# Batch 0's q and k in halves of the tokens, v's loads moved in the issue order, and the last block's two products swapped

## The chip, the cores and the metric

The kernel runs on one core of one Trainium2 chip. The metric is device time in microseconds, the median of several executions. The engines are TensorE (PE; its weight loads are PEld), VectorE (DVE), ScalarE (ACT), GpSimd (POOL) and SyncE (SP); each takes its own instructions in order. All loads are issued by GpSimd, because they convert float32 to bfloat16 on the way; nearly all stores are issued by SyncE.

## What is computed

Sliding-window attention with a linear bias for 8 batches, 8 heads, 576 tokens and 64 channels, and behind it a highway layer on the 4608 tokens of width 512:

```
scores = q k^T / 8 - slope[h] * |i - j|      for 0 <= i - j < 128, else masked
attn   = softmax(scores) v                   8 x 8 x 576 x 64
x      = attn as [8*576, 512]
H      = relu(x w_h);  T = sigmoid(x w_t + b_t)
out    = T * H + (1 - T) * x                 float32
```

## The kernel before

**Units and blocks.** A batch's attention is cut into 4 units of 128 keys (the last has 192), 32 units in all. Tokens go through the highway layer in 36 blocks of 128: four per batch, and one more for each pair of batches, made of the two remainders of 64.

**Steps.** The kernel is a list of small steps, written out by hand in the string `ORDER` (lines 28 to 37): each letter is a step, and the n-th occurrence of a letter is its n-th unit, block or load in the lists that `lists()` gives. The order of the letters is the order of the instructions on every engine; there are no loops beside it.

- `L`, `load`: one DMA issue on GpSimd. q and k of a batch go to the tiles `LD` (3 buffers of each), v to `VA`. Batch 0's q and k come in two parts each (the even and odd partitions, `j`), those of the others in four. v is one load per batch. The weights come in four parts each. The loads are in one list; at most 8 seem to be under way at a time: the ninth behind a load waits for it.
- `T`, `tr`: VectorE's 32 x 32 transposes of a batch's q (w = 0) or k (w = 1) from `LD` to `TR`.
- `V`, `copy_v`: two copies of v by VectorE to the other half of the partitions (`VC`).
- `s`, `scores`: TensorE; `e`, `soft`: ScalarE's exponent; `m`, `mask`: for eight of the units VectorE multiplies with a mask instead of adding it by matmuls.
- `p`, `pv`: attention times v on TensorE, with the sums in a column of ones; `n`, `norm`: VectorE's reciprocal and product; `x` and `c`: TensorE's transposition and ScalarE's copy.
- `h`, `mm_h`, and `z`, `mm_z`: the two products with the weights. `b`: ScalarE puts the bias into z's PSUM bank ahead of it; for the first and the last block a matmul does that.
- `u`, `relu_sub`: relu(h) - x in one step of VectorE from PSUM; or, for blocks in `RELU_S`, `r`, `relu`, on ScalarE and then `v`, `sub`, on VectorE from two-byte data.
- `a`: ScalarE's tanh; `y`: VectorE's scaling to the gate; `g`: the product with the gate; `o`, `add_x`: GpSimd adds x (for the last three blocks VectorE does, `f`); `d`: the store.
- `W`: TensorE multiplies zeros at the start. The digits are parts of the setup; `2` counts positions on GpSimd, `3` makes the bias, `4` the identity, `7` a copy of the bias for the batches' last units, `8` and `9` the mask.

VectorE's steps on two-byte data in SBUF (`m`, `V`, `v`, `y`, `g`) go through `locked`, and `add_x` on GpSimd waits for the last such step ahead of it in the order (`after`). Loads have no such wait.

PSUM has one buffer each for scores, P·V, h and z.

Of the kernel before, what the change touches and what calls it, by code (L numbers as in the profile page):

```python
# [9 lines left out]
P = 128  # L10
NB, NS = 8, 4
NLD, NTR, NVA, NVC, NP = 3, 3, 5, 3, 8


RELU_S = (5, 7, 8, 10, 11, 13, 14, 15, 16, 17, 19, 20, 22, 23, 25, 26, 28, 29, 31, 32, 33, 34, 35)
BIAS_S = (1, 2, 3, 4, 5, 6, 7, 8, 9, 10, 11, 12, 13, 14, 15, 16, 17, 18, 19, 20, 21, 22, 23, 24, 25, 26, 27, 28, 29, 30, 31, 32, 33, 34)

SUM_S = []
# [7 lines left out]
MASK_V = (1, 5, 9, 13, 17, 21, 25, 29)  # L26

ORDER = (
    "1LL62L3LL8L9LL7TLLLLTWWWWWWWWWseWWWWsLVeL4WWWpLsmLLneLWWWxLcLWWpsLnLLxhcepLuzLnLTLxahL5c"
    "bpTzyasgubonehLdxuLcsyLVzeLpnasLmLxhcLgbLpueLznLhTaLoxscbdupeznyxThcapbnrzgxoscapeLdhnLb"  # L30
    "VxscuLpezLnLhaLmLbxsTLrLczehygapvobsnrydxgzTcopayLdhbnLezyVxscyLvayLubLgpLeggLznLhoaTbxs"
    "ocdpeznodasmdbrvxTzchagyoprbhnedzguoxascVLdbpLeLznTaxscLbLpeLhvnzryyxvahycybprsnhegvzvoT"
    "rxasLdcgbpghenozmdrxasgocbpyLdeznLLhTaLxLrscbpezonxaydhvcVbpusnzeyxyhgcgmoapsrbodnhexvLd"
    "zgLcvLgpavLsrnobheyLdTxLzcLuopahnbLdzvrLyyxyaysVcbpgehonTrxdzcpasbnhegxyzgocupavdsvobnhe"
    "dmxzgcyropasndyxThcbpgrgzegonhoadxuscbVdpezonhaydyvbxvscyrpzenhgvmoxrscagdpgbhonezuodxas"
    "vcdybgpgeyohnzrodxahvdcgbpyorzndgaxvhcobprzdnyaxvhbygcgzorfhavddzyrgfavdygfd"
)

PARTS = [(2,) if b < 1 else (0, 1) for b in range(NB)]
WP, VP = 4, 1


def lists():

    units = [(b, s) for b in range(NB) for s in range(NS)]
    blocks = []
    for m in range(NB // 2):
        blocks += [(b, s) for b in (2 * m, 2 * m + 1) for s in range(NS)] + [(2 * m, NS)]  # L50
    trs = [(b, w) for b in range(NB) for w in range(2)]
    loads = []
    for b in range(NB):
        loads += [("t", b, w, j, i) for w in range(2) for j in range(2) for i in PARTS[b]]
        if b == 0:
            loads += [("v", 0, i) for i in range(VP)]
            loads += [("w", w, i) for w in (1, 0) for i in range(WP)] + [("w", 2, 0)]
        else:
            loads += [("v", b, i) for i in range(VP)]
# [12 lines left out]
    by["W"] = [()] * 100  # L72
    by["b"] = [n[i] for i in n if i in BIAS_S]
    return by
# [3 lines left out]
def kernel(  # L78
# [10 lines left out]
    nc = tc.nc  # L89
    B, H, S, D = q.shape  # L90
# [6 lines left out]
    U32 = mybir.dt.uint32  # L97
# [7 lines left out]
    NT = S // 16  # L105
# [13 lines left out]
    LD = {(i, w): cp.tile([P, NT, D], BF16, name=f"ld{i}{w}")  # L119
          for i in range(NLD) for w in range(2)}  # L120
# [22 lines left out]

    BL = cp.tile([P, 4, 384], BF16, name="bl")

    def load(kind, *at):
        if kind == "t":
            b, w, j, i = at
            n, i = (4, 0) if i == 2 else (2, i)
            nc.gpsimd.dma_start(  # L150
                out=LD[b % NLD, w][64 * i + j : 64 * i + 32 * n : 2].rearrange(
                    "p t d -> p (t d)"),
                in_=(q, k)[w][b, 4 * j + 2 * i : 4 * j + 2 * i + n].rearrange(
                    "g (s t) d -> (g s) (t d)", t=NT))
        elif kind == "v":
            b, i = at
            m = slice(36 // VP * i, 36 // VP * (i + 1))
            nc.gpsimd.dma_start(
                out=VA[b % NVA][:, m, 0:D],
                in_=v[b].rearrange("h s d -> (h s) d").rearrange("(m p) d -> p m d", p=P)[:, m])  # L160
        elif at[0] < 2:
            w, i = at
            c = slice(NC // WP * i, NC // WP * (i + 1))
            nc.gpsimd.dma_start(
                out=(wH, wT)[w][:, c, :],
                in_=(moe_w_h, moe_w_t)[w].rearrange("(c p) n -> p c n", p=P)[:, c, :])
# [65 lines left out]
        nc.tensor.matmul(out=pb[:], lhsT=ones0[:], rhs=bT[:], start=True, stop=True)  # L232
        nc.scalar.copy(out=bB[:], in_=pb[:])

    def tr(b, w):

        nc.vector.transpose(  # L237
            out=TR[b % NTR, w][:].rearrange("p n e -> p (n e)").bitcast(U32).rearrange(
                ("p (j s t) -> p t s j", "p (s t j) -> p t s j")[w], j=2, t=NT),
            in_=LD[b % NLD, w][:].rearrange("p t d -> p (t d)").bitcast(U32).rearrange(  # L240
                "p (t i) -> p t i", i=32))

    SC, PT, AV, RD, X = {}, {}, {}, {}, {}
# [177 lines left out]
    def mm_z(*at):  # L421
        begun = at in PZ
        if not begun:
            if lists()["z"].index(at) in LATE:
                PZ[at] = ps_sc.tile([P, G, 512], F32, name="sc")[:, 0, :]
            else:
                PZ[at] = ps_z.tile([P, DM], F32, name="z")[:]
            nc.tensor.matmul(out=PZ[at], lhsT=ones0[:], rhs=bT[:], start=True, stop=False)
        xt = XT[at]
        for c in range(NC):  # L430
            nc.tensor.matmul(out=PZ[at], lhsT=xt[:, c, :], rhs=wT[:, c, :],  # L431
                             start=False, stop=c == NC - 1, skip_group_check=begun)
# [39 lines left out]
    def store(b, s):  # L472
        ot = OT.pop((b, s))
        for i in range(1 + (s == NS)):
# [49 lines left out]
```

## Time and profile before

| | us |
|---|---|
| time, median of 3 runs | 159.09 (158.67 to 159.47) |
| the profiled execution | 160.06 |
| its span, first to last instruction | 158.3 |
| PE busy | 134.1 |
| DVE busy | 127.6 |
| ACT busy | 121.2 |
| POOL busy | 89.5 |

A row of the timeline gives start, length, engine, line, operation and names, the number of instructions that were merged into it, and in brackets the idle time of the engine before it with what ended it. A row of the chain of waits gives start, length and what the end of the program was waiting for in that time.

### The profile page before, as it was taken

The numbers are of one execution on the slowest core, as the hardware profiler recorded it, in microseconds if no ns is written. First come the engines' busy times: TensorE is split into PE (matmuls) and PEld (weight loads), VectorE is DVE, ScalarE is ACT, GpSimd is POOL, SyncE is SP. The second block draws the span as 40 slices with busy tenths as digits, with TensorE's granted clock in tenths as the row PEclk, the third lists the DMA queues.
The fourth block names the chain that finished last, engine by engine and source line by source line (L and its number), as shares of the span: only waits on it lengthen the run. The fifth ranks groups of instructions, "written<-read, shape, count | busy, mean of one in ns | idle before, by whom it ended". The sixth has DMA issues, their size and how long they took to land.

```text
span 158.3 us, 6992 instructions
## 1 busy us (share of the span) xinstructions
PE 134.1 (85%) x3096; PEld 73.7 (47%) x3096; DVE 127.6 (81%) x252; ACT 121.2 (77%) x176; POOL 89.5 (57%) x115
## 2 busy tenths in 40 slices
PE   0579897969997999699997999899699999999930
PEld 0114453544564565345654654465455555655310
DVE  5761629889949999998868589699999888997990
ACT  8353646677778979699988997987799698998730
POOL 7940967595249369926905592499404370766400
PEclk9999999999999999999999999999999999999996
DMA  3999999999969999996998589989993231145252
GB/s 57 168 161 178 203 197 139 182 233 156 183 164 147 169 201 203 169 200 215 193 157 135 149 148 157 136 188 220 201 175 117 93 133 70 72 137 197 73 201 66
DMA packets 46462, 25.09 MB, mean 159 GB/s; under 512 B 38752, under 2 KB 39776, under 8 KB 46432
## 3 DMA queue, kind: packets, MB, share of 16 engines
q0 software_dynamic: 41184, 15.21, 89.9%
q1 hardware_dynamic: 5168, 9.31, 16.9%
q8 instruction: 24, 0.39, 1.0%
q10 hardware_dynamic: 80, 0.13, 0.2%
q14 instruction: 6, 0.05, 0.1%
HBM read 30.41 MB, written 9.44 MB: 252 GB/s over the span
## 4 chain that ended last, share of the span: by engine, by line
PE 36%; DVE 31%; ACT 9%; issue 9%; DMA 6%; POOL 5%; DVEq 0%; POOLq 0%
PE h L398 10%; PE z L431 9%; DMA ld<-in_k_dram 6%; PE av L345 6%; DVE x L366 6%; DVE tr L237 6%; DVE tt L439 4%; DVE uu L443 4%; PE sc L302 4%; DVE uu L413 4%; ACT p L314 3%; PE av L380 3%; ACT xt L385 3%; DVE vc L321 3%; DVE uu L403 2%
## 5 line engine op out<-in xcount | busy, mean ns | idle before, releaser
L449 POOL TENSOR_TENSOR ot<-uu,x 128x512 f32<-128x512 bf16 x33 | 38.6, 1177 | 50.1 <-issue 16.6
L314 ACT ACTIVATE p<-sc 128x1536 bf16<-128x1536 f32 x32 | 46.5, 1452 | 7.1 <-PE sc L266 4.9
L398 PE MATMUL h<-wH,xt 128*128 128x512 bf16 x144 | 37.1, 380 | 0.5 <-DVE uu L403 0.3
L431 PE MATMUL z<-wT,xt 128*128 128x512 bf16 x140 | 36.1, 380 | 0.5 <-ACT z L419 0.3
L237 DVE STREAM_TRANSPOSE tr<-ld 128x1152 uint32<-128x1152 uint32 x16 | 29.4, 1850 | 2.3 <-DMA ld<-in_k_dram 1.5
L385 ACT COPY xt<-av 128x512 bf16<-128x512 bf16 x36 | 21.0, 583 | 11.1 <-PE av L380 10.9
L366 DVE TENSOR_TENSOR x<-av,rd 128x512 bf16<-128x512 f32 x36 | 24.9, 692 | 4.3 <-POOL ot L449 1.2
L345 PEld LDWEIGHTS <-p 64*128 64x128 bf16 (+1 forms) x1088 | 18.7, 96 | 16.2 <-issue 12.9
L436 ACT ACTIVATE tt<-z 128x512 f16<-128x512 f32 x35 | 21.0, 600 | 6.2 <-PE z L431 5.5
L345 PE MATMUL av<-va,p 64*128 64x65 bf16 (+1 forms) x544 | 21.5, 191 | 3.0 <-ACT xt L385 1.8
L345 PE MATMUL av<-vc,p 64*128 64x65 bf16 (+1 forms) x544 | 21.5, 192 | 0.8 <-DVE vc L321 0.8
L302 PE MATMUL sc<-tr,tr 32*64 32x192 bf16 (+2 forms) x1152 | 20.1, 254 | 2.4 <-DVE tr L237 1.2
L419 ACT COPY z<-bB 128x512 f32<-128x512 f32 x34 | 20.4, 599 | 0.4
L398 PEld LDWEIGHTS <-xt 128*128 128x128 bf16 x144 | 12.5, 97 | 13.5 <-issue 2.0
L431 PEld LDWEIGHTS <-xt 128*128 128x128 bf16 x144 | 12.5, 97 | 12.9 <-issue 0.9
L380 PE MATMUL av<-ident,x 128*128 128x128 bf16 x144 | 14.1, 221 | 4.9 <-DVE x L366 3.2
L302 PEld LDWEIGHTS <-tr 32*64 32x64 bf16 x1152 | 14.6, 136 | 7.3 <-issue 2.4
L150 POOL DMA_DIRECT2D ld<-in_k_dram x30 | 15.7, 535 | 3.9 <-DMA wH<-in_moe_w_h_dram 1.4
L380 PEld LDWEIGHTS <-x 128*128 128x128 bf16 x144 | 9.5, 97 | 17.2 <-DVE x L366 13.2
L443 DVE TENSOR_TENSOR uu<-uu,tt 128x512 bf16<-128x512 bf16 x36 | 16.4, 476 | 0.3
L150 POOL DMA_DIRECT2D ld<-in_q_dram x30 | 15.8, 548 | 1.0 <-POOLq L508 0.8
L365 DVE RECIPROCAL rd<-av 128x8 f32<-128x8 f32 x36 | 7.2, 201 | 10.6 <-PE av L345 10.4
(50 smaller groups left out, 136.3 us busy)
## 6 DMA issues: line engine op xcount, KB each, us to landing
out_dram<-ot SPq DMA_DIRECT2D x32, 256.0 KB, 2.5
va<-in_v_dram POOLq DMA_DIRECT2D x8, 576.0 KB, 10.8
ld<-in_q_dram POOLq DMA_DIRECT2D x28, 144.0 KB, 8.8
ld<-in_k_dram POOLq DMA_DIRECT2D x28, 144.0 KB, 5.6
out_dram<-ot SPq DMA_DIRECT2D x7, 128.0 KB, 3.7
ld<-in_q_dram POOLq DMA_DIRECT2D x2, 288.0 KB, 4.4
ld<-in_k_dram POOLq DMA_DIRECT2D x2, 288.0 KB, 6.6
wT<-in_moe_w_t_dram POOLq DMA_DIRECT2D x4, 128.0 KB, 9.6
```

The costliest lines, as they stand in the source:

```text
L150: nc.gpsimd.dma_start(out=LD[b % NLD, w][64 * i + j : 64 * i + 32 * n : 2].rearrange("p t d -> p (t d)"), in_=(q, k)[w][b, 4 * j + 2 * i : ...
L237: nc.vector.transpose(out=TR[b % NTR, w][:].rearrange("p n e -> p (n e)").bitcast(U32).rearrange(("p (j s t) -> p t s j", "p (s t j) -> p ...
L302: nc.tensor.matmul(out=sc[j * D : (j + 1) * D, g, off : off + n], lhsT=KT[rows, a * D : (a + 1) * D, j, e], rhs=QT[rows, a * D : a * D + n ...
L314: nc.scalar.activation(out=t[:, :, :, 0:192], in_=SC.pop((b, s))[:, :, 0:384].rearrange("p g (i n) -> p g i n", i=2), func=ACTF.Exp, scale ...
L345: nc.tensor.matmul(out=av[o : o + n, j, g * (D + 1) : (g + 1) * (D + 1)], lhsT=PT[bb, ss][rows, g].rearrange("p i n -> p (i n)")[:, at : a ...
L366: nc.vector.tensor_tensor(out=x[:].rearrange("p (j g d) -> p j g d", j=2, d=D), in0=av[:, :, :, 0:D], in1=rd[:].to_broadcast([P, 2, G, D]) ...
L380: nc.tensor.transpose(out=x_part(at)[:, c // 2, (c % 2) * P : (c % 2 + 1) * P], in_=X[at][:, c * P : (c + 1) * P], identity=ident[:])
L385: nc.scalar.copy(out=xt[:].rearrange("p (j c) n -> p j (c n)", j=2), in_=x_part(at))
L398: nc.tensor.matmul(out=pa, lhsT=xt[:, c, :], rhs=wH[:, c, :], start=c == 0, stop=c == NC - 1)
L431: nc.tensor.matmul(out=PZ[at], lhsT=xt[:, c, :], rhs=wT[:, c, :], start=False, stop=c == NC - 1, skip_group_check=begun)
L443: locked(nc.vector.tensor_tensor(out=UU[at][:], in0=UU[at][:], in1=TT.pop(at)[:], op=ALU.mult))
L449: op = nc.gpsimd.tensor_tensor(out=ot[:], in0=uu[:], in1=x[:], op=ALU.add)
```

## The change

1. Batch 0's q and k are loaded in two halves of the tokens each (288 tokens, `SPLIT = (0, 1)`); the second halves land in the buffers `LD[2, w]`, which are free then. The load order is first half of q, first half of k, v, second half of q, second half of k, then the bias of z, then the weights. Each half has its own transposes (`tr` takes a third index, and the list `T` has 18 entries instead of 16).
2. `ORDER` is new as a whole. At the start the identity (`4`) comes ahead of the bias (`3`), ten zero matmuls come ahead of the mask, and the copy `7` behind the first exponent. The issues of v for batches 2 to 7 stand at other places among VectorE's steps.
3. For the last block z comes ahead of h, and block 35 leaves `RELU_S`: its relu and subtraction are one step of VectorE (`u`), ahead of the product `g`, instead of `r` on ScalarE and `v` on VectorE.

```diff
-RELU_S = (5, 7, 8, 10, 11, 13, 14, 15, 16, 17, 19, 20, 22, 23, 25, 26, 28, 29, 31, 32, 33, 34, 35)
+RELU_S = (5, 7, 8, 10, 11, 13, 14, 15, 16, 17, 19, 20, 22, 23, 25, 26, 28, 29, 31, 32, 33, 34)
...
 ORDER = (
-    "1LL62L3LL8L9LL7TLLLLTWWWWWWWWWseWWWWsLVeL4WWWpLsmLLneLWWWxLcLWWpsLnLLxhcepLuzLnLTLxahL5c"
-    "bpTzyasgubonehLdxuLcsyLVzeLpnasLmLxhcLgbLpueLznLhTaLoxscbdupeznyxThcapbnrzgxoscapeLdhnLb"
...
-    "vcdybgpgeyohnzrodxahvdcgbpyorzndgaxvhcobprzdnyaxvhbygcgzorfhavddzyrgfavdygfd"
+    "1LL26L43LLLTWWWWWWWWWW8LLTL9LLWWWsLeLV7LWWWWpLTLnWWWsLTexLLcsmLLpeLznLLLLxasc5pbLhnezuLx"
+    "ahLcTLbLzLLpaLTusyghneouxdcsyLyVheLpbnsLmLxzcLuLpagLhnbLeozuTxdscabypeznTaxhcbgpryyoznsa"
...
+    "bpuezndhgayyoxrscgdbpveohnydxgzgcorpahnobdrxyzdvcgpoahnbdyrxvzgcfzavdyhgafydugfd"
 )
...
-WP, VP = 4, 1
+WP, VP, SPLIT = 4, 1, (0, 1)
...
-    trs = [(b, w) for b in range(NB) for w in range(2)]
...
+    half = [(3, 4) if w in SPLIT else (2,) for w in range(2)]
+    trs = [(0, w, half[w][0]) for w in range(2)] + [(0, w, i) for w in range(2) for i in half[w][1:]]
+    trs += [(b, w, 2) for b in range(1, NB) for w in range(2)]
+    loads = [("t", 0, w, j, half[w][0]) for w in range(2) for j in range(2)]
+    loads += [("v", 0, i) for i in range(VP)]
+    loads += [("t", 0, w, j, i) for w in range(2) for i in half[w][1:] for j in range(2)]
+    loads += [("w", 2, 0)] + [("w", w, i) for w in (1, 0) for i in range(WP)]
+    for b in range(1, NB):
         loads += [("t", b, w, j, i) for w in range(2) for j in range(2) for i in PARTS[b]]
...
+        loads += [("v", b, i) for i in range(VP)]
...
+    def part(b, w, i):
+
+        return LD[b % NLD, w][:] if i < 3 else LD[2 * (i - 3), w][:, 0 : NT // 2]
+
     def load(kind, *at):
         if kind == "t":
             b, w, j, i = at
+            if i > 2:
+                rows = slice((i - 3) * S // 2, (i - 2) * S // 2)
+                nc.gpsimd.dma_start(
+                    out=part(b, w, i)[j:P:2].rearrange("p t d -> p (t d)"),
+                    in_=(q, k)[w][b, 4 * j : 4 * j + 4, rows].rearrange(
+                        "g (s t) d -> g s (t d)", t=NT // 2))
+                return
...
-    def tr(b, w):
-
+    def tr(b, w, i):
+
+        n, h = (1, 0) if i < 3 else (2, i - 3)
         nc.vector.transpose(
             out=TR[b % NTR, w][:].rearrange("p n e -> p (n e)").bitcast(U32).rearrange(
-                ("p (j s t) -> p t s j", "p (s t j) -> p t s j")[w], j=2, t=NT),
-            in_=LD[b % NLD, w][:].rearrange("p t d -> p (t d)").bitcast(U32).rearrange(
+                ("p (j h s t) -> p h t s j", "p (h s t j) -> p h t s j")[w],
+                j=2, h=n, t=NT // n)[:, h],
+            in_=part(b, w, i).rearrange("p t d -> p (t d)").bitcast(U32).rearrange(
                 "p (t i) -> p t i", i=32))
```

In the new order the copy of v of batch 1 still stands ahead of the issue of v of batch 2. The rows around the issues of v, as the two orders have them on VectorE (numbers are units for `m`, blocks otherwise): before, `V1` / issue 2; `n8` / issue 3 / `V2`; `n11` / issue 4 / `y6 V3`; `n14` / issue 5 / `n15`; `T60` / issue 6 / `n20`; `n24` / issue 7 / `y19 y20`. After, `V1` / issue 2 / `n4`; `V2` / issue 3 / `u6 n8`; `u9` / issue 4 / `V3`; `T50` / issue 5 / `n16`; `T60` / issue 6 / `u18`; `V6` / issue 7 / `n26`.

More of the change, by code (lines that the diff above doesn't have):

```diff
@@ L28 @@
 ORDER = (
-    "1LL62L3LL8L9LL7TLLLLTWWWWWWWWWseWWWWsLVeL4WWWpLsmLLneLWWWxLcLWWpsLnLLxhcepLuzLnLTLxahL5c"
-    "bpTzyasgubonehLdxuLcsyLVzeLpnasLmLxhcLgbLpueLznLhTaLoxscbdupeznyxThcapbnrzgxoscapeLdhnLb"
[L31 to L35, printed above, removed]
-    "vcdybgpgeyohnzrodxahvdcgbpyorzndgaxvhcobprzdnyaxvhbygcgzorfhavddzyrgfavdygfd"
+    "1LL26L43LLLTWWWWWWWWWW8LLTL9LLWWWsLeLV7LWWWWpLTLnWWWsLTexLLcsmLLpeLznLLLLxasc5pbLhnezuLx"
+    "ahLcTLbLzLLpaLTusyghneouxdcsyLyVheLpbnsLmLxzcLuLpagLhnbLeozuTxdscabypeznTaxhcbgpryyoznsa"
+    "gLdVLbLxhcepuzLnLaLTxsocbphednzrvxmscavpybyhnezggrgoxTscLdpevLyhnLLasgLubLxezhcVLapLbson"
+    "rzeTodxhcodapsnrLdbLmxzcvvpayyhnbezyuxghcgToasbLdpeLznLLrxTLascbpehonzrgLdgxLahyVLcLbpLr"
+    "znoaxscydvobpehndzgrvmoxascbvdpvezyynhaggxrsTocbpLdvezLnLhTaLxscbopeuzndhaVbxsycyyrypzen"
+    "hyggxamoscbpgdrvozenhodTaxsLcdubLvpLeghLnozryLxdagsLgcgLbvpLeznoxahVLdcbprznohTaodbxscdp"
+    "euznhayyxmscrvpybhenzgvrToxascbdypgeoznhaydgbxouscpgdeohnsrvdVzevxhgcmapsnobrzvdyxgahyco"
+    "bpuezndhgayyoxrscgdbpveohnydxgzgcorpahnobdrxyzdvcgpoahnbdyrxvzgcfzavdyhgafydugfd"
 )
 PARTS = [(2,) if b < 1 else (0, 1) for b in range(NB)]
-WP, VP = 4, 1
+WP, VP, SPLIT = 4, 1, (0, 1)
 def lists():
@@ L50, in lists @@
         blocks += [(b, s) for b in (2 * m, 2 * m + 1) for s in range(NS)] + [(2 * m, NS)]
-    trs = [(b, w) for b in range(NB) for w in range(2)]
-    loads = []
-    for b in range(NB):
-        loads += [("t", b, w, j, i) for w in range(2) for j in range(2) for i in PARTS[b]]
[L55 to L59, printed above, removed]
+    half = [(3, 4) if w in SPLIT else (2,) for w in range(2)]
[6 more added lines that the diff above has]
+    for b in range(1, NB):
+        loads += [("t", b, w, j, i) for w in range(2) for j in range(2) for i in PARTS[b]]
+        loads += [("v", b, i) for i in range(VP)]
     by = dict(L=loads, T=trs, V=list(range(NB)))
```

## The prediction

> **What bounds the kernel now.** I read the page first, then the chain of waits over the first 36 us, then the timeline of single engines at the start, around three of the v issues and at the end. The page:
>
> ```profile
> span 158.3 us, 6992 instructions
> PE 134.1 (85%) x3096; PEld 73.7 (47%) x3096; DVE 127.6 (81%) x252; ACT 121.2 (77%) x176; POOL 89.5 (57%) x115
> ...
> PE   0579897969997999699997999899699999999930
> ...
> PE 36%; DVE 31%; ACT 9%; issue 9%; DMA 6%; POOL 5%; DVEq 0%; POOLq 0%
> ```
>
> No engine alone sets the time. The chain alternates between TensorE and VectorE, and each is busy over 80% of the span. The holes are at the start, where TensorE has three poor slices (4 us each), and at the end. The profiled execution took 160.06 us: its span and 1.76 around it. That is 0.97 over the median, 159.09, of the three timed runs; I work out differences on the trace and take them off 159.09.
>
> The chain of waits for the first 36 us (start, us, what):
>
> ```profile
> 3.61 7.06 DMA ld<-in_k_dram
> ...
> 12.20 0.87 PE sc L302 x31
> ...
> 16.11 1.46 ACT p L314
> ...
> 17.62 0.59 PE sc L302 x28
> ...
> 29.43 0.51 PE sc L302 x29
> ...
> 30.27 0.98 PE h L398 x4
> ...
> 32.18 0.47 DVE vc L321
> ...
> 32.67 1.86 DVE vc L321
> ...
> 34.58 0.41 PE av L345 x15
> ```
>
> Three things set the first third. The first scores wait for all of k of batch 0 (10.67). From 12.2 to 31.25 the chain is TensorE's and ScalarE's own work. Then the first P·V of batch 1, unit 4 (I call it p4), waits for the copies of v, of which the second took 1.86 us where the first took 0.47. The timeline of GpSimd says why:
>
> ```profile
> 15.61 0.53 POOL L164 DMA_DIRECT2D wH<-in_moe_w_h_dram  x1 [4.12 <-DMA va<-in_v_dram]
> ...
> 31.89 0.51 POOL L150 DMA_DIRECT2D ld<-in_k_dram  x1 [0.48 <-DMA va<-in_v_dram]
> 32.38 1.85 POOL L158 DMA_DIRECT2D va<-in_v_dram  x1
> ```
>
> GpSimd waits until v of batch 1 has landed (31.87), issues the last part of k of batch 2, and at 32.38 begins the issue of v of batch 2, 1.85 us. VectorE's copy that starts after 32.38 ends only after 34.23. The copy that had started before it, at 32.18, kept its 0.47 us across 32.38. So an issue of v holds two-byte steps that start behind it, and not one already running.
>
> **Part 1, batch 0 in halves.** The rows of VectorE and TensorE at the start:
>
> ```profile
> 4.97 1.15 DVE L207 SCALAR_TENSOR_TENSOR bt<-rel,sl,far 128x384 bf16<-128x384 f32 x2
> ...
> 6.97 2.34 DVE L237 STREAM_TRANSPOSE tr<-ld 128x1152 uint32<-128x1152 uint32 x1 [0.85 <-DMA ld<-in_q_dram]
> ...
> 10.76 1.38 DVE L237 STREAM_TRANSPOSE tr<-ld 128x1152 uint32<-128x1152 uint32 x1 [1.46 <-DMA ld<-in_k_dram]
> ...
> 15.35 1.05 DVE L321 COPY vc<-va 64x1170 bf16<-64x1170 bf16 x2 [3.20 <-DMA va<-in_v_dram]
> ...
> 16.43 0.27 DVE L213 TENSOR_SCALAR ident<-rel_i 128x128 bf16<-128x128 int32 x1
> ...
> 16.73 0.20 PE L345 MATMUL av<-va,p 64*128 64x65 bf16 x1
> ```
>
> q landed at 6.9, k 3.7 us later and v 4.6 us after k. The first halves of q and k are together as many bytes as q alone, so they land at about 6.9, v 4.6 us later at 11.5, and the second halves where v landed, 15.3, since the bytes up to there are the same. VectorE's setup ends at 6.1 and now takes the identity, 0.27, too: 6.4. The half transposes cost between half and all of a whole one: 1.9 to 3.7 us for the pair; I take near half, 2.0, since the rows are 1152 elements long. The scores of unit 0, at 12.2 before, then need only be through by 12.6, and the first P·V comes at 11.5 + 1.05 + 0.1 = 12.7 instead of 16.73. Now VectorE waits for the second half of q (13.4, half of 3.7 behind v), with the normalisation of unit 0 queued behind that wait and TensorE's transposition waiting for it, and then for k's (15.3). With q's half transposed at 14.6 come scores of unit 1, about 0.9, and their exponent, 1.46: 17.0. Scores have one PSUM buffer, so those of unit 2 start then, having begun at 17.62 before. The 4 us at the first P·V are 0.6 us there.
>
> The extra cost, four more issues on GpSimd at about 0.5 each and two more transposes, lies in holes: GpSimd sat 4.12 us in the row above, VectorE 1.46 and 3.20. Without that cover it would be 2.1 us on GpSimd and up to 1.8 on VectorE.
>
> **What is late next** is batch 1. Its loads stand behind the same bytes, so v of batch 1 lands at 31.87 as before, and p4 cannot start before 31.87 + 2 × 0.47 + 0.04 = 32.85. TensorE and VectorE have to be ready by then:
>
> ```profile
> 25.02 3.52 DVE L237 STREAM_TRANSPOSE tr<-ld 128x1152 uint32<-128x1152 uint32 x2
> 28.46 0.24 DVE L439 TENSOR_SCALAR tt<-tt 128x512 f16<-128x512 f16 x1
> ...
> 31.27 0.69 DVE L403 SCALAR_TENSOR_TENSOR uu<-h,x 128x512 bf16<-128x512 f32 x1 [0.67 <-PE h L398]
> ```
>
> Batch 1's two transposes ran from 25.02 to 28.46 and waited for no load; in the new order they stand behind the same steps (the normalisation of unit 2 and the first h), which come no later, so 28.46 is the late end. From 28.46 to the copies VectorE took 3.72 with 0.67 of waiting in it: 3.05, and the new order adds one scaling of 0.29. It is ready at 31.8, just ahead of 31.87. TensorE does scores of 4 (0.84, from 29.43 to the next row), h of 2 (0.98), transposition of 3 (0.4, the row at 147.53 below), scores of 5 and h of 3 between: 4.0, from 28.5 to 32.5, and with a wait like the 0.67 above 33.1. I take p4 at 33.1 against 34.58: **1.5 us gained**; the ends are 1.73 (32.85) and 0 (the copy is held again).
>
> **Part 2, v's issues.** The stall of 32.67 is not alone:
>
> ```profile
> 59.55 1.85 POOL L158 DMA_DIRECT2D va<-in_v_dram  x1
> ...
> 109.52 1.91 POOL L158 DMA_DIRECT2D va<-in_v_dram  x1
> ```
> ```profile
> 59.83 1.68 DVE L439 TENSOR_SCALAR tt<-tt 128x512 f16<-128x512 f16 x1
> ...
> 62.50 0.29 DVE L439 TENSOR_SCALAR tt<-tt 128x512 f16<-128x512 f16 x1
> ...
> 109.69 2.22 DVE L439 TENSOR_SCALAR tt<-tt 128x512 f16<-128x512 f16 x4
> ```
>
> The step that takes 0.29 took 1.68 beside one issue, and four of them took 2.22 beside another: 1.4 and 1.1 us held. By the new order the issues for batches 3, 5 and 6 stand beside transposes, normalisations and an h step of four-byte data; those for batches 4 and 7 stand close to the copies of batches 3 and 6, two-byte steps. So two stalls go and two of the same size can come. Both rows' stalls were on the chain, but everything between is re-ordered as well, and no row of before shows how. I book nothing, with ends of 2.5 us either way: the two stalls shown, removed or added.
>
> Between p4 and the last P·V (p35) both orders put 61 groups of h and z on TensorE and 31 normalisations on VectorE (31 h and 30 z before, 30 and 31 after), so what is gained at p4 is kept at p35, apart from those 2.5.
>
> **Part 3, the last block.** The chain's row of the last P·V (p35), and TensorE, GpSimd and VectorE at the end:
>
> ```profile
> 145.90 0.51 PE av L345 x48
> ```
> ```profile
> 147.53 0.40 PE L380 MATMUL av<-ident,x 128*128 128x128 bf16 x4 [0.16 <-DVE x L366]
> ...
> 150.55 0.38 PE L428 MATMUL sc<-bT,ones 128*128 128x512 bf16 x1
> ...
> 150.77 1.03 PE L431 MATMUL sc<-wT,xt 128*128 128x512 bf16 x4
> ```
> ```profile
> 149.13 1.60 POOL L449 TENSOR_TENSOR ot<-uu,x 128x512 f32<-128x512 bf16 x1 [2.35 <-DVE uu L443]
> ```
> ```profile
> 149.74 1.28 DVE L413 TENSOR_TENSOR uu<-rr,x 128x512 bf16<-128x512 bf16 x1
> ...
> 152.98 0.43 DVE L443 TENSOR_TENSOR uu<-uu,tt 128x512 bf16<-128x512 bf16 x1
> 153.44 0.69 DVE L454 TENSOR_TENSOR ot<-uu,x 128x512 f32<-128x512 bf16 x1
> ```
>
> Behind the last transposition (ends 147.93) before did h34, z34, h35, bias and z35, to 151.8, then tanh, scaling, product, sum, to 154.13. After, h34 stands ahead of the transposition, where TensorE waited; behind it come z34 (0.98, like the h row above), bias and z35 (1.25, from 150.55 to 151.80), h35 (0.98): 151.1. The tanh and the scaling run beside h35; then relu minus x in one step on VectorE (0.69, of the kind of L403 above), product 0.43, sum 0.69, less two overlaps of 0.1 each and plus 0.3 since VectorE comes from block 34's sum: 153.0. GpSimd's last add stands four steps earlier, so the step it held (1.28 instead of 0.42) is free. **1.1 us gained**; the ends are 0.2 (the held step comes back) and 1.3.
>
> **Sum:** 1.5 + 0 + 1.1 = 2.6 us, 159.09 − 2.6 = **156.5 us** (157.5 for an execution like the profiled one). Its own range is 155.0 to 158.0.
>
> **Rivals.** *The copy is held again* (20%). VectorE is ready at 31.8, v lands at 31.87: with 0.1 us more the second copy starts behind GpSimd's issue, p4 is at 34.6 and only the end's 1.1 is left: 158.0. For it: the margin is thin. Against: that estimate starts from the late end of the transposes. [...]
>
> *The stalls go in the middle too* (12%): 2.5 us more, 154.0. For it: both rows are on the chain. Against: TensorE is busy over nine tenths in most middle slices.
>
> *The loads come too late for the transposes* (20%), the one that ends slower. The new order issues the last q part of batches 4, 5 and 7 only two blocks ahead of the transpose, GpSimd's adds being queued ahead of it; a block takes (145.9 − 34.6)/31 = 3.6 us, so 7.2 us.
>
> ```profile
> ld<-in_q_dram POOLq DMA_DIRECT2D x28, 144.0 KB, 8.8
> ```
>
> At the median of 8.8 each of the three holds VectorE's queue, normalisations behind it, for 1.6 to 1.8 us: 5.4 in all, 5.4 − 2.6 = 2.8 slower, 161.9. It decides from a landing time over 7.2 us, and is even with before at 8.1. Against: parts issued later stand behind fewer others, and the 8.8 comes from a queue that was full.
>
> *It does not come through* (13%): the middle's new order costs what start and end give, 159.1, since VectorE is busy eight tenths whatever the order.
>
> **Numbers.** The forecast has 35%. About 0.5%, 0.8 us, is what a measurement of this kernel can tell from no change. Forecast, held copy and freed stalls are faster (67%); the fourth is the same, with a little of the held copy's upper and the late loads' lower edge: 12% in all; the rest of the late loads and of the middle's bad orders 21%. The range from 154.2 to 160.8 leaves out half of the freed stalls (6%) and those late loads that cost the whole 2.8 (14%).
>
> **What would show it.** Right: first P·V at about 12.7, scores of unit 2 by 16.7, both copies of batch 1 at 0.47 each from 31.9, p4 at 33; from p35 to the end of the last sum 7.1 us instead of 8.2; 111 us between p4 and p35. Wrong: a copy of over 1 us at 32 (rival one), transposes of batches 4, 5 or 7 that wait for a load (rival three), or more than 114 us from p4 to p35. If v of batch 1 lands later than 32.5, halved pieces made the loads slower, and part 1 fails at its root.

## The result, and the profile after

The changed kernel takes 165.51 us (median; 163.0 to 165.96), the kernel before in the same comparison 159.28 (158.67 to 159.76). The ratio is 1.032, with a 95% interval from 1.023 to 1.041: slower by 3.2%, where 156.5 us had been forecast. Executions of one kernel differ here by up to 4% (three of 214 to 700 us aside), and the ratios compare the fast executions of both kernels alone, so they can differ a little from the quotient of two medians.

The page of the changed kernel:

```profile
span 163.4 us, 6970 instructions
PE 134.4 (82%) x3060; PEld 75.5 (46%) x3095; DVE 123.7 (76%) x254; ACT 120.7 (74%) x175; POOL 92.2 (56%) x119
...
PEclk9985555999999999999999999999999999999997
```

TensorE has as much work as before (134.4 us against 134.1) in a span that is 5.1 us longer, so the time is waiting. The clock is halved from 10.9 to 28.0 us, by the trace's own record of it. The page of the kernel before shows no such stretch, but its record begins only at 15.44, and where there is no record the views print a full clock. The kernel before has products of zeros on both sides of that time:

```profile
6.96 4.02 PE L392 MATMUL h<-zero 128*128 128x512 bf16 x9
...
15.97 0.82 PE L392 MATMUL h<-zero 128*128 128x512 bf16 x3
```

The nine start 0.43 us apart, the three 0.22. So TensorE was at half clock up to about 15.4 in the kernel before; in the changed one it was so up to 4.1 and again from 10.9 to 28.0.

I cut the span at two marks that both kernels have: VectorE's normalisation of block 4 (it starts when the first P·V of batch 1, p4, ends) and that of block 35 (the end of p35).

| | start, to block 4 | middle, to block 35 | end, to the last sum |
|---|---|---|---|
| before | 35.02 | 111.45 | 7.66 |
| after | 40.61 | 112.17 | 6.45 |
| difference | +5.59 | +0.72 | -1.21 |

The middle and the end came as forecast. All of the loss lies in the first 40 us, where a gain of 1.5 us had been expected. VectorE's rows there (start, length, instruction, and in brackets the idle time ahead with what ended it), of the changed kernel:

```profile
8.87 1.20 DVE L251 STREAM_TRANSPOSE tr<-ld 128x576 uint32<-128x576 uint32 x1 [2.24 <-DMA ld<-in_q_dram]
12.16 0.78 DVE L251 STREAM_TRANSPOSE tr<-ld 128x576 uint32<-128x576 uint32 x1 [2.09 <-DMA ld<-in_k_dram]
17.67 0.94 DVE L336 COPY vc<-va 64x1170 bf16<-64x1170 bf16 x2 [4.73 <-DMA va<-in_v_dram]
...
38.63 0.94 DVE L336 COPY vc<-va 64x1170 bf16<-64x1170 bf16 x2 [0.40 <-DMA va<-in_v_dram]
...
40.61 0.21 DVE L380 RECIPROCAL rd<-av 128x8 f32<-128x8 f32 x1 [1.03 <-PE av L360]
```

The first half of q, with half of the bytes, was there 1.9 us later than the whole of q before (its transpose starts at 8.87 against 6.97), and the first half of k later than the whole of k (12.16 against 10.76). v of batch 0 came 2.3 us later, v of batch 1 6.8 us later (38.63 against 31.87). The copies of batch 1's v are clean, 0.94 for the two, but late.

The bytes moved per 4 us are in the last column of the windows view (busy times by engine before it, then the granted clock and the DMA share). Before:

```profile
4.00:8.00 4.00, 2.36 (x19) 0.74 (x19) 3.08 (x6) 1.60 (x4) 4.00 (x6) 1.00 1.01 164
8.00:12.00 4.00, 2.97 (x7) 0.76 (x5) 2.54 (x2) 2.06 (x4) 1.72 (x4) 1.00 1.81 162
```

After:

```profile
4.00:8.00 4.00, 2.56 (x23) 0.76 (x21) 2.53 (x6) 1.42 (x4) 4.00 (x5) 1.00 0.69 79
8.00:12.00 4.00, 0.00 (x0) 0.00 (x0) 1.20 (x1) 0.70 (x1) 1.79 (x4) 0.86 1.80 141
```

The loads ran at half the rate between 4 and 8 us. The single transfers say how: of the loads' data packets (one for each of a load's 64 pieces) the trace shows 15, 20 and 18 under way at 3.0, 3.5 and 4.0 us before, and 4, 4 and 4 after; a packet has 4608 bytes before and 2304 after, and takes 367 and 192 ns at the median. While q's first load was alone, four pieces at a time moved. GpSimd then shows what became of that:

```profile
11.36 0.58 POOL L177 DMA_DIRECT2D wT<-in_moe_w_t_dram  x1 [1.81 <-DMA ld<-in_k_dram]
...
17.93 1.33 POOL L177 DMA_DIRECT2D wT<-in_moe_w_t_dram  x2 [5.04 <-DMA va<-in_v_dram]
...
27.62 1.87 POOL L171 DMA_DIRECT2D va<-in_v_dram  x1 [0.23 <-issue]
```

With eight loads under way GpSimd waits for the oldest, 5.04 us for v alone. The rate stays behind: 149, 131 and 170 GB/s in the three windows from 12 to 24 us, where before had 180, 200 and 198. v of batch 1 is issued at 27.62. Before, that issue stood at 22.34:

```profile
22.34 1.88 POOL L158 DMA_DIRECT2D va<-in_v_dram  x1
```

At the end, GpSimd's last add, VectorE's step that it held before (1.28 us), and the last sum:

```profile
152.26 1.15 POOL L464 TENSOR_TENSOR ot<-uu,x 128x512 f32<-128x512 bf16 x1 [1.07 <-issue]
...
155.41 0.42 DVE L428 TENSOR_TENSOR uu<-rr,x 128x512 bf16<-128x512 bf16 x1
...
158.54 0.69 DVE L469 TENSOR_TENSOR ot<-uu,x 128x512 f32<-128x512 bf16 x1
```

### The profile page after: what moved, and what is told of

It reads as the page before. It is cut to its first block, busy times and chain, and to the rows that moved or that the text cites. A ratio compares the mean times of both kernels' runs of the same rounds, so it can differ in the third digit from the quotient of the medians.

```text
span 163.4 us, 6970 instructions
## 1 busy us (share of the span) xinstructions
PE 134.4 (82%) x3060; PEld 75.5 (46%) x3095; DVE 123.7 (76%) x254; ACT 120.7 (74%) x175; POOL 92.2 (56%) x119
## 3 DMA queue, kind: packets, MB, share of 16 engines
q0 software_dynamic: 43040, 15.22, 90.2%
## 5 line engine op out<-in xcount | busy, mean ns | idle before, releaser
L329 ACT ACTIVATE p<-sc 128x1536 bf16<-128x1536 f32 x32 | 46.5, 1453 | 16.0 <-PE sc L281 11.5
L446 PE MATMUL z<-wT,xt 128*128 128x512 bf16 x120 | 35.4, 389 | 2.1 <-ACT z L434 0.6
L413 PE MATMUL h<-wH,xt 128*128 128x512 bf16 x130 | 34.8, 380 | 1.8 <-issue 1.1
L251 DVE STREAM_TRANSPOSE tr<-ld 128x1152 uint32<-128x1152 uint32 (+1 forms) x18 | 29.7, 1658 | 4.4 <-DMA ld<-in_q_dram 2.2
L317 PE MATMUL sc<-tr,tr 32*64 32x192 bf16 (+2 forms) x1152 | 21.8, 260 | 9.4 <-DVE tr L251 5.0
L360 PEld LDWEIGHTS <-p 64*128 64x128 bf16 (+1 forms) x1088 | 19.2, 98 | 16.0 <-issue 10.9
L360 PE MATMUL av<-va,p 64*128 64x65 bf16 (+1 forms) x544 | 22.3, 193 | 2.9 <-DMA va<-in_v_dram 1.4
L360 PE MATMUL av<-vc,p 64*128 64x65 bf16 (+1 forms) x544 | 22.2, 194 | 0.9 <-DVE vc L336 0.8
L317 PEld LDWEIGHTS <-tr 32*64 32x64 bf16 x1152 | 15.3, 137 | 15.8 <-issue 6.9
L395 PEld LDWEIGHTS <-x 128*128 128x128 bf16 x144 | 9.9, 100 | 14.9 <-DVE x L381 9.4
L163 POOL DMA_DIRECT2D ld<-in_k_dram x28 | 14.7, 544 | 2.7 <-DMA va<-in_v_dram 1.3
L163 POOL DMA_DIRECT2D ld<-in_q_dram x28 | 14.6, 544 | 1.5 <-DMA wT<-in_moe_w_t_dram 1.5
L171 POOL DMA_DIRECT2D va<-in_v_dram x8 | 15.0, 1879 | 0.7 <-issue 0.7
```

The lines of the kernel that those rows point to most:

```text
L163: nc.gpsimd.dma_start(out=LD[b % NLD, w][64 * i + j : 64 * i + 32 * n : 2].rearrange("p t d -> p (t d)"), in_=(q, k)[w][b, 4 * j + 2 * i : ...
L251: nc.vector.transpose(out=TR[b % NTR, w][:].rearrange("p n e -> p (n e)").bitcast(U32).rearrange(("p (j h s t) -> p h t s j", "p (h s t j) ...
L317: nc.tensor.matmul(out=sc[j * D : (j + 1) * D, g, off : off + n], lhsT=KT[rows, a * D : (a + 1) * D, j, e], rhs=QT[rows, a * D : a * D + n ...
L329: nc.scalar.activation(out=t[:, :, :, 0:192], in_=SC.pop((b, s))[:, :, 0:384].rearrange("p g (i n) -> p g i n", i=2), func=ACTF.Exp, scale ...
L360: nc.tensor.matmul(out=av[o : o + n, j, g * (D + 1) : (g + 1) * (D + 1)], lhsT=PT[bb, ss][rows, g].rearrange("p i n -> p (i n)")[:, at : a ...
L395: nc.tensor.transpose(out=x_part(at)[:, c // 2, (c % 2) * P : (c % 2 + 1) * P], in_=X[at][:, c * P : (c + 1) * P], identity=ident[:])
```

## The theory and its rivals

**The theory: narrow loads.** A whole load takes four heads of 16 rows, and those 64 rows lie at one step in memory, so they are one dimension of 64. Half a head's tokens are 16 shorter rows, and from one head to the next the step is another: the same 64 rows are 4 x 16, with an outer step of 4. Such a load is moved four pieces at a time, and all that is queued behind it comes late.

**The rivals.** Halves are slow because there are more loads of shorter pieces; the new order of the steps, not the loads, makes the start late; the half clock from 10.9 to 28.0 us, with TensorE idle from 8 to 13, does; or the loss belongs to the end or the middle.

## The experiments

Marks are the starts of the normalisations of blocks 4 and 35, in us, from one profiled execution each; "start", "middle" and "end" are as in the table above, and "profiled execution" is the time of that one execution. Line numbers differ by a few from kernel to kernel.

| kernel | v of batch 1 copied at | start | middle | end | profiled execution | median | ratio to before, 95% |
|---|---|---|---|---|---|---|---|
| before | 32.18 | 35.02 | 111.45 | 7.66 | 160.06 | 159.28 | |
| after | 38.63 | 40.61 | 112.17 | 6.45 | 165.14 | 165.51 | 1.023 to 1.041 |
| halves alone | 38.44 | 39.95 | 110.95 | 7.83 | 164.64 | 164.47 | 1.021 to 1.032 |
| whole loads | 35.95 | 38.61 | 112.45 | 6.46 | 163.50 | 161.27 | 0.990 to 1.003 |
| whole loads, warm | 37.63 | 39.11 | 113.40 | 6.46 | 164.89 | 161.58 | 1.002 to 1.020 |
| halves, warm | 38.90 | 41.57 | 113.29 | 6.46 | 167.19 | 166.74 | 1.034 to 1.048 |
| by group | 37.42 | 38.85 | 112.29 | 6.46 | 163.59 | 163.75 | 1.012 to 1.031 |
| eight loads | 33.25 | 34.77 | 113.94 | 7.66 | 162.29 | 161.17 | 1.001 to 1.011 |
| whole, narrow | 36.94 | 38.82 | 111.55 | 7.67 | 163.99 | 163.93 | 1.020 to 1.032 |
| halves, wide | 32.77 | 34.72 | 111.59 | 6.46 | 158.66 | 159.00 | 0.993 to 1.003 |
| swap alone | 32.05 | 34.72 | 112.45 | 7.92 | 161.00 | 160.11 | 0.993 to 1.002 |
| swap, v later | 32.37 | 33.88 | 114.12 | 7.93 | 161.94 | 161.06 | 0.999 to 1.009 |
| end alone | 31.74 | 33.25 | 114.95 | 6.45 | 160.54 | 161.34 | 0.995 to 1.009 |
| end, v later | 31.81 | 33.70 | 117.88 | 6.45 | 163.94 | 161.43 | 0.995 to 1.008 |

The kernel before was run beside each group: 160.44, 160.22 and 159.98 us (medians of the three groups).

How far a mark moves by itself can be read from three rows. Before, swap alone and end alone have the same loads and the same order up to the last blocks, yet block 4 stands at 35.02, 34.72 and 33.25. Differences of 1 to 2 us at the start therefore say little, and the executions profiled for whole loads, whole loads warm and the end with the later v took 2.2, 3.3 and 2.5 us more than their kernels' medians.

**Halves alone.** The kernel before, its order too, with the half loads, the changed kernel's list of loads and the half transposes; the copy of batch 0's v moves up by one step with them:

```diff
 # before's ORDER, with the first line
-"1LL62L3LL8L9LL7TLLLLTWWWWWWWWWseWWWWsLVeL4WWWpLs..."
+"1LL62L3LL8L9LL7TLLLLTWWWWWWWWWseWWWWVTsLeL4TWWWpLLLLLs..."
```

> The kernel before, with the half loads and half transposes put into its own order, its v issues and its last block unchanged. Theory A: the loads alone bring the loss, v of batch 1 lands at 37 to 39; 163 to 167 us (no gain at the end here). Rival C (the new order): 158.5 to 160.5 us.

164.47 us, and the start is 4.9 us later than before. The new order and the end are not needed for the loss: the halves bring it alone.

**Whole loads in the new order.** The changed kernel with `SPLIT` empty, and without the letters of the extra loads and transposes in `ORDER`:

```diff
-WP, VP, SPLIT = 4, 1, (0, 1)
+WP, VP, SPLIT = 4, 1, ()
```

> The changed kernel with batch 0's q and k loaded and transposed whole again (SPLIT empty), all else in the new order. Theory A: v of batch 1 lands at 32 as before, the end keeps its 1.2 us; 157.5 to 159.5 us. Rival C (the new order): 163 or more. Rival D (TensorE's clock, at half from 11 to 28 us in the changed kernel, is what costs): the early zero matmuls stay, TensorE idles from 8 to 12, so the clock falls again and 161 or more.

161.27 us, ratio 0.996: the loss goes with the halves. v of batch 1 lands at 32.5 (issued at 21.90, 10.6 us to landing), near the 31.6 that the same reading gives for before (22.34 and 9.3). The start is still 3.6 us late in the profiled execution, which at 163.50 is not typical. It has a half clock from 9.4 to 26.5 us and a copy of v that is held, 2.17 for the pair beside the next v's issue; how much each costs there is not shown.

```profile
35.95 2.17 DVE L336 COPY vc<-va 64x1170 bf16<-64x1170 bf16 x2
...
35.83 2.03 POOL L171 DMA_DIRECT2D va<-in_v_dram  x1
```

**The clock.** The changed kernel with 35 more products of zeros in the holes of the start, and the whole loads with 26:

```diff
-LLTWWWWWWWWWW8LLTL9LLWWWsLeLV7LWWWWpLTLnWWWsLTex...
+LLTWWWWWWWWWW8LLTL9LLWWWWWWWWWWWWWWWWWWWWWWWsLeLV7LWWWWWWWWWWWWpLTLnWWWWWWsLTexWWWW...
```

> The changed kernel with 35 more matmuls of zeros in TensorE's holes of the first 23 us, so that its clock stays up. Theory A: v of batch 1 still lands at 38 to 39 us, so the time stays within 1.5 us of the changed kernel's 165 us. Rival D (the half clock costs): 160 to 161.5 us, since 4 us of TensorE's work at half clock between 24 and 28 and as much before it are made good.

> The whole-load kernel in the new order, with 26 more matmuls of zeros in TensorE's holes between 8 and 16 us. In the whole-load kernel the loads come as before (v of batch 1 issued at 21.9) and the clock stands at half from 10.7 to 27 us; the third normalisation is 3.6 us later than before. If the clock is what it lacks: third normalisation at 24 to 25, p4 at 33 to 35, 157 to 159 us and a narrow spread. If the new order of the middle or start lacks something else: 160 or more with the clock up.

The clock in the page of the halves with more zeros (halves, warm):

```profile
PEclk9999789999999999599999999999999999999996
```

With the halves the clock was full from about 5 us on but for one window at the start (18.9 to 22.3). The normalisation of block 2 stood at 30.7, no earlier than in the changed kernel (30.1). v of batch 1 landed at 36.8 (issued at 26.31, 10.5 us to landing), 1.8 earlier than there and 5.2 later than before; VectorE came to copy it at 38.90, and the pair took 2.17 beside the next issue. The time was no better: 166.74. So the half clock is not what the change costs. With whole loads the clock was full until 28.0 and the normalisation of block 2 stood at 24.8 instead of 27.8, as expected, but the first h then waited for a transfer (GpSimd's last part of batch 1's k):

```profile
27.86 0.49 PE L413 MATMUL h<-wH,xt 128*128 128x512 bf16 x1 [2.31 <-DMA ld<-in_k_dram]
```

It is the fourth product of that block's h, which needs the fourth part of w_h. In the trace that part had landed at 20.1; it signals the same semaphore as the last part of k, which landed at 27.5, since the loads use eight semaphores in turn. Why the product waited for the later of the two I haven't settled. Block 4 came no earlier (39.11), in an execution of 164.89, and the median stayed at 161.58.

**Halves in more loads.** The changed kernel with each half of q or k in four loads by groups of two heads, each with 16 rows as its outer step:

```diff
-loads = [("t", 0, w, j, half[w][0]) for w in range(2) for j in range(2)]
+loads = [("t", 0, w, j, half[w][0]) for w in range(2) for j in range(4)]
...
-out=part(b, w, i)[j:P:2]..., in_=(q, k)[w][b, 4 * j : 4 * j + 4, rows].rearrange(
-    "g (s t) d -> g s (t d)", t=NT // 2))
+out=part(b, w, i)[32 * j : 32 * j + 32]..., in_=(q, k)[w][b, j : 8 : 4, rows].rearrange(
+    "j (s t) d -> s j (t d)", t=NT // 2))
```

> The changed kernel, but each half of batch 0's q and k in four loads by group of heads (32 partitions, 16 rows of tokens as the outer step in memory) instead of two by parity (64 partitions, 4 heads as the outer step). Same halves, same piece of 2304 bytes, eight more issues of about 0.5 us. Theory A (the half loads are slow because of their outer step of 4: 79 GB/s from 4 to 8 us against 164 before, and all later loads stand behind them): first halves land by 7.5, v by 12.5, v of batch 1 by 32.5; 157 to 160 us. Rival B (short pieces are slow as such): no better than 163. Rival C (the new order of the middle is what costs): no better than 163 though the loads land early.

The first halves did land early (transposed at 6.57 and 8.81), but the time was 163.75, and v of batch 1 came at 37.4. This miss did not tell the theories apart: with sixteen small loads GpSimd stands with work unissued, waiting for a place among the eight under way:

```profile
15.33 0.79 POOL L157 DMA_DIRECT2D ld<-in_k_dram  x1 [3.79 <-DMA va<-in_v_dram]
```

**Eight loads at full width.** The kernel before with batch 0's q and k in eight loads of 64 pieces of 2304 bytes, as in the changed kernel, but cut so that the 64 rows make one dimension:

```diff
+t = slice((i - 3) * NT // 2, (i - 2) * NT // 2)
+nc.gpsimd.dma_start(out=LD[b, w][j:P:2, t]...,
+    in_=(q, k)[w][b, 4 * j : 4 * j + 4].rearrange("g (s t) d -> (g s) t d", t=NT)[:, t]...)
```

> The kernel before, with q and k of batch 0 in eight loads of the same number, bytes and pieces (64 partitions, 2304 bytes each) as the changed kernel's, but with one outer step of 64 rows in memory instead of 4 heads by 16 rows; whole transposes, v behind all eight. If the outer step of 4 slows the changed kernel's halves: 155 GB/s or more from 4 to 8 us as before, k complete by 11.5, 158 to 160.5 us. If short pieces or the number of loads against the limit of eight in flight slow them: 110 GB/s or less from 4 to 8, 162 us or more.

```profile
4.00:8.00 4.00, 2.35 (x19) 0.74 (x19) 2.06 (x5) 1.59 (x4) 4.00 (x6) 1.00 0.95 153
```

153 GB/s in the window 4 to 8 us where the changed kernel had 79, and 171, 197 and 195 from 12 us on. v of batch 1 is copied at 33.25 and block 4 stands at 34.77, as early as before. The time is 161.17, a ratio of 1.001 to 1.011: eight loads cost about 0.6%, not the 3.2% of the change. Number and length of the pieces are not the cause.

**Whole loads made narrow.** The kernel before, in which nothing changes but the step from row to row within a head, 35 tokens instead of 36. The 64 rows then are 4 x 16 (batch 0 reads overlapping tokens):

```diff
+rows = (q, k)[w][b, 4 * j : 4 * j + 4].rearrange("g (s t) d -> g s (t d)", t=NT)
+rows = bass.AP(rows.tensor, rows.offset, [rows.ap[0], [(NT - 1) * D, 16], rows.ap[2]])
+nc.gpsimd.dma_start(out=LD[b % NLD, w][j:P:2].rearrange("p t d -> p (t d)"), in_=rows)
```

> The kernel before, in which the four loads of batch 0's q and k read rows of 36 tokens that begin 35 tokens apart within a head, not 36, so that batch 0 reads overlapping tokens and its output isn't the reference's. Number of loads, bytes, length and partitions of a piece and the order of the steps are those of before; only the 64 rows don't make one dimension any more, but 4 x 16. Theory A (the outer step of 4 is what costs): under 100 GB/s in the slice 4:8 where before had 164, q landed after 8.5 instead of 6.9 us, over 1000 packets of 4 bytes in the first 30 us where before had 373, v of batch 1 at 35 or later instead of 31.9, time 3 to 7 above before. Theory B (the shape of the rows makes no difference): rates and time as before, within 0.8.

```profile
4.00:8.00 4.00, 2.06 (x18) 0.71 (x19) 2.35 (x5) 1.30 (x4) 3.93 (x5) 1.00 0.71 105
```
```profile
12.38 2.34 DVE L244 STREAM_TRANSPOSE tr<-ld 128x1152 uint32<-128x1152 uint32 x1 [5.96 <-DMA ld<-in_q_dram]
```

The same four loads, bytes, pieces and order: q lands at 12.38 instead of 6.9, block 4 stands 3.8 us later, and the time is 163.93, 3.95 above before. The rate between 4 and 8 us is 105 GB/s, just over the 100 expected, and 12 in the first 4 us, where before had 61. Of the data packets 4, 4 and 5 were under way at 3.0, 3.5 and 4.0 us. The outer step alone costs what a narrow load costs.

**Halves made wide.** The changed kernel, every step and load of it, but a half is now the first or last 18 tokens of each run of 36, so that the rows make one dimension of 64 (batch 0's tokens come in another order than the reference's):

```diff
-in_=(q, k)[w][b, 4 * j : 4 * j + 4, rows].rearrange("g (s t) d -> g s (t d)", t=NT // 2))
+in_=(q, k)[w][b, 4 * j : 4 * j + 4].rearrange(
+    "g (s t) d -> (g s) t d", t=NT)[:, t].rearrange("p t d -> p (t d)"))
```

> The changed kernel, with other tokens in the two halves of batch 0's q and k: a half is the first (or last) 18 tokens of every run of 36, instead of the first (or last) 288 tokens, so batch 0's tokens come in another order than the reference's. Number of loads, bytes, the 2304 bytes of each of the 64 partitions and the order of the steps are those of the changed kernel. What differs is that the 64 rows now lie at one step in memory and make one outer dimension of 64, where they made 4 x 16. Theory A (the outer step of 4 makes a half load narrow, and what is queued behind it late): over 140 GB/s in the slices 4:8 and 8:12 as in the kernel before (164 and 162), where the changed kernel had 79 and 141; first halves transposed at 7 to 9 us, first copy of v by 13 (17.7 in the changed kernel), v of batch 1 by 33.5 (38.6), the normalisation of block 4 at 33.5 to 36.5 (40.6), time 156 to 160.5. Theory B (halves as such, their number, or their new order make the loads late): v of batch 1 at 37 or later and the time within 1.5 of the changed kernel's 165.5. In between, 160.5 to 164: the loads come early, but the order of the steps holds the middle.

```profile
4.00:8.00 4.00, 2.82 (x23) 0.83 (x21) 3.58 (x7) 1.74 (x4) 4.00 (x6) 1.00 0.99 119
```
```profile
6.22 1.21 DVE L251 STREAM_TRANSPOSE tr<-ld 128x576 uint32<-128x576 uint32 x1
7.78 0.78 DVE L251 STREAM_TRANSPOSE tr<-ld 128x576 uint32<-128x576 uint32 x1 [0.35 <-DMA ld<-in_k_dram]
13.10 1.05 DVE L336 COPY vc<-va 64x1170 bf16<-64x1170 bf16 x2 [4.54 <-DMA va<-in_v_dram]
...
32.77 0.94 DVE L336 COPY vc<-va 64x1170 bf16<-64x1170 bf16 x2
...
34.72 0.21 DVE L380 RECIPROCAL rd<-av 128x8 f32<-128x8 f32 x1 [1.00 <-PE av L360]
```

159.00 us instead of 165.51: with the width back, the whole loss is gone. The rate (119 GB/s) is below the 140 expected, but 50 came in the first 4 us already, where the changed kernel had 6. Together with the narrow whole loads this is the proof both ways: width taken from before makes it slow, width given to after makes it as fast as before.

The Trainium skill, DMA: Bandwidth & Descriptors, section "Why a DMA increments its semaphore by 16 and not by 1", says that a transfer, some direct copies issued by GpSimd excepted, runs on the largest number of engines, up to 16, that divides the slowest dimension of both its access patterns. Here that is 64 rows against 64 partitions for a whole load, 4 heads against 64 partitions for a half. The trace agrees: 4 pieces under way with the outer step of 4, in two kernels, and 13 to 20 with 64, in three others (the kernel before; eight loads, 15, 18 and 15; halves made wide, 13, 19 and 18), where two loads can be under way at once. The trace counts pieces; it does not name the engines that move them.

**The end.** First the swap of block 35 alone, in the kernel before:

```diff
-RELU_S = (... 33, 34, 35)
+RELU_S = (... 33, 34)
-ORDER: ...gzorfhavddzyrgfavdygfd
+ORDER: ...gzorfzavddhygafydugfd
```

> The kernel before with the last block's z ahead of its h and its relu and subtraction as one step of VectorE, nothing else; GpSimd's last add stays where it was and still holds one step. The prediction's own ends: 0.2 to 1.3 us faster, 0.5 likeliest; in the changed kernel, from the last normalisation to the end of the last sum took 6.4 us against 7.6. Rival (the middle and the end give nothing): within 0.2 us.

The end took 7.92, no less than before: GpSimd's last add still stands beside VectorE's step.

```profile
149.84 1.60 POOL L449 TENSOR_TENSOR ot<-uu,x 128x512 f32<-128x512 bf16 x1 [2.37 <-DVE uu L443]
...
150.44 1.27 DVE L413 TENSOR_TENSOR uu<-rr,x 128x512 bf16<-128x512 bf16 x1
```

Then the changed kernel's order of steps from the P·V of block 34 on, put behind the kernel before, alone and with the next v's load one place later:

```diff
-ORDER: ...hvdcgbpyorzndgaxvhcobprzdnyaxvhbygcgzorfhavddzyrgfavdygfd
+ORDER: ...hvdcgbyzgorpahnobdrxyzdvcgpoahnbdyrxvzgcfzavdyhgafydugfd
 # and for the second kernel
+i = loads.index(("v", 2, 0))
+loads[i], loads[i + 1] = loads[i + 1], loads[i]
```

> The kernel before, with the changed kernel's order of steps from the P.V of block 34 on, z of block 35 ahead of its h and its relu by VectorE with it; start, loads and middle are those of before. Theory A (the 1.2 us at the end came from the whole end's order, the earlier sum of block 32 on GpSimd with it): from the normalisation of block 35 to the end of the last sum 6.4 to 6.8 us instead of 7.6, the step that GpSimd held 0.42 instead of 1.27, time 0.8 to 1.3 below before. Theory B (the last P.V comes later by what the end saves, since more steps stand ahead of it): normalisation of block 35 0.7 to 1.5 later and no difference in time.

> The kernel of the end alone, and with it the load of v of batch 2 one place later in the list of loads, behind the first q part of batch 3, so that its issue no longer holds the second copy of v of batch 1. If both gains stand alone and add up: the second copy 0.47 to 0.6 instead of 1.86, normalisation of block 4 about 0.7 to 1.1 earlier than before, from the normalisation of block 35 to the end 6.4 to 6.8 instead of 7.6, time 1.5 to 2.3 below before, and the fastest of all kernels run. Rival (what is gained at block 4 is lost in the middle, by a shorter or longer hole of TensorE that halves its clock there): normalisation of block 35 no earlier than in the kernel with the end alone, and its time.

> The tail-alone kernel, with the first part of q of batch 3 issued ahead of v of batch 2 instead of behind it: GpSimd's long issue then begins at 32.9 instead of 32.4, behind the start of VectorE's second copy of v (32.67). If the held copy was on the path as the chain of waits says: the copy takes 0.47 instead of 1.86, p4 at 33.2 instead of 34.6, and up to 1.4 us more off than the tail alone, less 0.3 for the mask step that then meets the issue. If something else is late next: as the tail alone.

With the whole order the end takes 6.45, as in the changed kernel, so it takes the order of the whole end, with the earlier add in it, to free the step. But the P·V of blocks 34 and 35 came later: from the normalisation of block 33 to that of 35 it took 7.48 against 6.02 before. TensorE first waits for the bias of z, ahead of P·V:

```profile
143.64 1.02 PE L431 MATMUL z<-wT,xt 128*128 128x512 bf16 x4 [0.57 <-ACT z L419]
```

What the end saves is taken ahead of it, and the ratio is 1.002. The 1.8 us by which block 4 came earlier in that execution are gone by block 33 as well (140.71 against 140.45). In the changed kernel, whose order differs further up, the same stretch takes 5.79, so there the gain is net; what in that order makes it so I haven't taken apart.

Moving the next v's issue alone (the kernel with the swap) gave both copies clean:

```profile
32.37 1.02 DVE L323 COPY vc<-va 64x1170 bf16<-64x1170 bf16 x2 [0.96 <-DMA va<-in_v_dram]
```

But the end alone, where that issue was not moved, has both clean as well:

```profile
31.74 1.02 DVE L321 COPY vc<-va 64x1170 bf16<-64x1170 bf16 x2 [0.64 <-DMA va<-in_v_dram]
...
32.48 1.85 POOL L158 DMA_DIRECT2D va<-in_v_dram  x1
```

There VectorE stood waiting for v, and its second copy began ahead of the issue; in the kernel before VectorE reached the copies at 32.18, and the second, at 32.67, began behind the issue at 32.38. So a few tenths of a us in one execution decide whether the copy is held, and block 4 at 33.88 is not shown to be the moved issue's doing. No time is won either: the middle is 2.7 us longer in this execution and 6.4 in that of the end with the later v, each with a window of half clock (58.5 to 62.0 and 71.3 to 74.8), but 3.5 in the end alone, which has no such window (the slower last two blocks are 1.5 of the 6.4 and of the 3.5). What takes an early block 4 back again is open. The medians, 161.06 and 161.43, show no gain, and none of these versions is measurably faster than the kernel before.

## Why the prediction was wrong, point by point

**The step that failed** is the first of part 1: that the first halves of q and k, being together as many bytes as q alone, land at about 6.9. They landed at 8.87 and 12.16. I reasoned by bytes, as if the queue had one rate; the rate hangs on the access pattern, and the one line of the diff that says it (`g s (t d)` for `(g s) (t d)`) I read as the same rows. All later numbers of part 1 hang on that, with "its loads stand behind the same bytes, so v of batch 1 lands at 31.87 as before" among them: it landed at 38.63. The text named that very sign as its root failure, at 32.5, but no rival carried it with a price. Four narrow loads cost 3.8 us at block 4, the changed kernel's eight 5.6.

**With that step repaired** the halves made wide show what the rest of part 1 is worth. v of batch 0 came at 13.10, not 11.5, and the copies of batch 1 at 32.77, not 31.9, each at half of 0.94 as forecast. Scores of unit 2 came at 18.11, not by 16.7:

```profile
13.12 0.19 PE L360 MATMUL av<-va,p 64*128 64x65 bf16 x1 [2.63 <-DMA va<-in_v_dram]
...
18.11 0.88 PE L317 MATMUL sc<-tr,tr 32*64 32x192 bf16 x32 [1.03 <-ACT p L329]
```

P·V may start earlier than at 16.73, but TensorE is idle ahead of it, and the clock is half from 14.9 to 21.7 in that execution. Block 4 stood 0.3 us earlier than before, where 1.5 were forecast. The same start steps gave 33.25 to 35.02 in three executions, so 0.3 is not told from nothing. That v of batch 0 and the scores of unit 2 came 1.6 and 1.4 us later than forecast speaks for a gain below 1.5 at full width too. The sum by the runs is 0.3 at the start, -0.1 in the middle and 1.2 at the end, 1.4 us by the spans (158.3 and 156.9). The median of 159.00 stands 0.98 below before's, within an interval (0.993 to 1.003) that can't tell it from no change.

**Part 2** came out, in part by luck: the two copies of v of batch 1 kept 0.47 each, but in two kernels with the changed kernel's order (whole loads; halves, warm) the pair took 2.17, so the order does not secure it. The middle, booked at nothing with 2.5 us either way, came out 0.7 longer.

**Part 3** was right: from p35 to the end of the last sum 7.03 us (152.20 to 159.23), where 7.1 stood against 8.2 before, and the step held by GpSimd fell from 1.28 to 0.42. The chain of waits of the changed kernel has p35 as

```profile
152.20 0.55 PE av L360 x45
```

The swap alone gains nothing at the end (7.92); with the earlier add it is 6.45. The earlier add without the swap was not run.

**The rivals.** The copy was not held in the changed kernel. The loads of batches 4, 5 and 7 made no transpose wait: of the 4.4 us of all waits ahead of transposes, 4.33 are the two at 8.87 and 12.16.

```profile
L251 DVE STREAM_TRANSPOSE tr<-ld 128x1152 uint32<-128x1152 uint32 (+1 forms) x18 | 29.7, 1658 | 4.4 <-DMA ld<-in_q_dram 2.2
```

So the rival that ended slower looked at late loads in the wrong place.

## What to carry to other kernels

When a load is cut, look at the dimension that it is left with outermost, not at its bytes: 64 rows that merge to one dimension moved 13 to 20 pieces at a time, the same 64 rows as 4 x 16 moved four. A narrow load at the head of a queue cost more here than its own delay, because GpSimd waits for a place behind it: 1.9 us at the first half of q had grown to 6.8 us at v of batch 1. A mark read from one execution needs its own spread beside it, too: block 4 moved by 1.8 us with nothing changed ahead of it. To tell what an edit is worth apart from such a side effect, keep the edit and restore the one property that went with it, even where the data are then in another order.

## What the runs showed of the hardware

Each narrow load brought about 190 packets of 4 bytes more: in the first 30 us there were 373 before, 1120 with four narrow loads (747 / 4 = 187) and 1922 with eight (1549 / 8 = 194), and 426 with the halves made wide. The page's queue of the loads has 41184 packets before and 43040 after. Of the 1856 packets between the two, 1600 have 4 bytes, and 256 come from pieces that are cut in two. What the short packets are for, and whether they cost time beside the width, no run here separates.

In these traces the half clock comes in whole windows: stretches of 3.4, 6.8, 10.2, 13.7 and 17.1 us, 1 to 5 times 3.41, each with a hole of TensorE of 1.2 to 5.5 us at or just ahead of its start. The Trainium skill, TensorE: Matmul & The Clock Gate, section "What's actually happening", gives a free-running window of 3413 ns and says that the point of the change varies with it; the stretches agree with the length. One such window in the middle (58.5 to 62.0, 59.1 to 62.5, 71.3 to 74.8) came in some kernels with the same middle order as before and not in others, and stands beside middles that are 2.5 to 6.4 us longer. The end alone has a middle 3.5 us longer without one, so the window is not shown to be what makes them long.
